# Two-part f32r queries and keys in row pairs, P @ V in halves, and keys loaded one by one, in a kernel of two gated attentions

## The chip, the cores and the metric

The kernel runs on one core of a Trainium2 chip. The metric is the time of one execution on the device, in microseconds (us). The profile is one execution taken by the hardware profiler. Its engines are PE (TensorE: matrix products, with weight loads shown apart as PEld), DVE (VectorE), ACT (ScalarE), POOL (GpSimd) and SP (SyncE, which here issues nearly all DMAs). A name such as L560 is line 560 of the kernel before.

## The reference

A sequence of 2048 tokens of width 512 passes through two attentions of 32 heads with 16 columns each, and the two results are mixed by a gate that belongs to the token.

```python
g = sigmoid((x * gate_w).sum(-1))                 # gate of a token
# A: full attention, no mask
q, k, v = heads(x @ wqkv)                         # 32 heads of 16
a = softmax(q @ k^T * 0.25) @ v @ wo_a            # 2048 x 2048 scores a head
# B: four segments of 512 tokens, each causal, with a running memory
for s in range(4):
    p = softmax(qs @ ks^T * 0.25 + causal_mask)   # 512 x 512
    a_mem = (phi(qs) @ M) / (phi(qs) @ z + 1e-6)
    o_s = sigmoid(beta) * a_mem + (1 - sigmoid(beta)) * (p @ vs)
    M, z = M + phi(ks)^T @ vs, z + sum(phi(ks))
b = concat(o_s) @ wo_b
out = g * a + (1 - g) * b
```

All tensors are float32, and the result has to be of float32 quality.

## The kernel before

**Parts of a number.** PE takes float32 slowly, so a float32 factor is split into parts of fewer bits, and a product is a sum over pairs of parts. In the projections both factors are two f32r parts (`h` and `l`), and three products (l·h, h·l, h·h) make one. In the scores q and k are each three bf16 parts, and the pairs of parts are laid out along the rows of one product: 16 rows for each of six pairs, 96 in all, and three more rows in which q carries the negative row maximum in three parts and k carries ones. A score product thus has 99 rows and gives the score less its row's maximum.

**Projections.** They run in slots (`slot`, L247). A slot is the twelve products (L250) of one tile, and it has four places at which posted functions run. For A there are four chunks of 512 tokens with twelve slots each: four tiles of q, four of k, four of v. B follows with the same slots. A tile of q or k (`qk_tile`, L283) is an octet of heads by 512 tokens. ACT writes its first part as `q1` (L294), DVE forms the rest (L301), ACT writes the second part `q2` (L307), DVE or POOL the third, `q3` (L315), and each part is stored to scratch in DRAM (`qd`, `kd`) by a DMA of its own (L295, L308, L316). The buffers of the parts are two deep. For B, phi of the tile is formed too and goes into the memory's products (`mem_q`, `mem_den`, `mem_k`). `load_gate` loads x by rows, and DVE forms the gate's logits beside A's slots; the gate's sigmoid (L401) and the DMAs that spread it (L404 to L407) come between A's and B's projections.

**Units and steps of the attention.** A unit is a group of four heads and a chunk of 512 queries. A has 8 groups by 4 chunks with 16 steps each (a step is a block of 128 keys), 512 steps. B has 32 units with 4 steps each, whose products are 512, 384, 256 and 128 columns wide because of the causal mask. The loop over steps is written out in order. A step runs four scores (`score_parts`, L560), each followed by an exponential on ACT (L563) into the tile `p`; one step of row maxima (`max_parts`) that runs ahead, by 22 steps in A and by 12 in B (`lead`); and P @ V (`values`, L579) of a step two (A) or three (B) steps back. The products of the maxima (L174 in A, L185 in B) have queries on the partitions, and DVE reduces each along its keys (L176, L190). When a unit's maxima are complete, `finish_max` splits them in parts on POOL, and `transpose_max` brings them into rows by a product (L154), an ACT copy (L156) and a DMA into the unit's q tile (L157). Scores have three PSUM banks, maxima three, P @ V one. P @ V has four heads in four column strips of the array; each product is in float32 and shows as two records in the profile. A score and a product of a maximum alternate on PE: score, maximum, score, maximum, and at the end of the step P @ V. At the end of a unit ACT copies the P @ V bank (L583) and SP stores it (L586).

**Loads.** All of the following go through SP's queue, in the order of the program. A unit's q tile takes three loads (`load_q`, L116 to L118), a key tile three (`load_k`, L125 to L127), of 48, 32 and 19 rows for k and 48, 32 and 16 for q. The row copies that the pairs need are made by these loads, for k with a repeated source. `loads` issues what a step of the maxima needs five steps (`PRE`) ahead. In A the four key tiles of a group are issued together with the first q tile of the group, ahead of it; in B a unit has one key tile and one q tile. There are buffers for six q tiles and eight key tiles. After each octet of A, its 2 MB of sums and inverse row sums are loaded (`a_load`) and stored again, scaled.

**Beside the steps.** Lists by step (`at`, `filler`) hold the scaling of A's and B's results and the output projection (L721), whose products run between the scores of B's steps. The first 22 steps of maxima run beside B's projections: `some_max` runs one product in places 1 and 3 of each slot from B's fourth slot (n = 3) on, and `loads(0)` ahead of B's first slot issues the first four key tiles and the first q tile.

Of the kernel before, what the change touches and what calls it, by code (L numbers as in the profile page):

```python
# [10 lines left out]
F32 = mybir.dt.float32  # L11
F32R = mybir.dt.float32r
BF16 = mybir.dt.bfloat16
# [27 lines left out]
def gated_mix(ctx, tc, x, xT, wqkv, a_wo, b_wq, b_wk, b_wv, b_wo, beta, gate_w, out):  # L41
# [3 lines left out]
    # ---------------------------------------------------------------- scratch in DRAM  # L45
    dr = ctx.enter_context(tc.tile_pool(name="dr", bufs=1, space=DRAM))
    # rows (split, d), heads of an octet, tokens of a chunk; three rows of ones below those of k
    qd = {}
    kd = {}
    for side in "AB":  # L50
        for o in range(NO):
            for c in range(NCH):
                qd[side, o, c] = dr.tile([48, 8, CH], BF16, name=f"qd{side}{o}{c}")
                kd[side, o, c] = dr.tile([51, 8, CH], BF16, name=f"kd{side}{o}{c}")
# [7 lines left out]
    # 32 rows a head: 16 of P @ V, then the sum of P  # L62
# [6 lines left out]
    # ---------------------------------------------------------------- constants  # L69
# [3 lines left out]
    identb = const.tile([128, 128], BF16, name="identb")  # L73
    nc.vector.tensor_copy(identb, identf)
# [15 lines left out]
    ones = const.tile([24, CH], BF16, name="ones")  # L90
# [4 lines left out]
    # ---------------------------------------------------------------- pools of the attention  # L95
# [7 lines left out]
    steps = []          # of the scores  # L103
# [6 lines left out]

    def load_q(u):
# [4 lines left out]
        nc.sync.dma_start(t[0:48], src[:, hs])  # L116
        nc.sync.dma_start(t[48:80], src[0:32, hs])
        nc.sync.dma_start(t[80:96], src[0:16, hs])  # L118
        qt[u] = t

    def load_k(side, g, c):
        t = kp.tile([128, 4, CH], BF16, tag="k", name=f"k{side}{g}{c}")
        src = kd[side, g // 2, c]
        hs = slice(4 * (g % 2), 4 * (g % 2) + 4)
        nc.sync.dma_start(t[0:48], src[0:16, hs].unsqueeze(0).broadcast_to([3, DH, 4, CH]))  # L125
        nc.sync.dma_start(t[48:80], src[16:32, hs].unsqueeze(0).broadcast_to([2, DH, 4, CH]))  # L126
        nc.sync.dma_start(t[80:99], src[32:51, hs])  # L127
        kt_[side, g, c] = t

    # ------------------------------------------------ row maxima, queries on partitions  # L130
    pmt = {}
    late = []           # (step of the maxima at which to run, function)

    def finish_max(u):
# [6 lines left out]
        ms = mp.tile([128, 3, 4, 4], BF16, tag="ms", name="ms")  # L141
        r1 = mp.tile([128, 4, 4], F32, tag="r1", name="r1")
        r2 = mp.tile([128, 4, 4], F32, tag="r2", name="r2")
        nc.gpsimd.tensor_copy(ms[:, 0], nm)  # L144
        nc.gpsimd.tensor_sub(r1, nm, ms[:, 0])
        nc.gpsimd.tensor_copy(ms[:, 1], r1)
        nc.gpsimd.tensor_sub(r2, r1, ms[:, 1])
        nc.gpsimd.tensor_copy(ms[:, 2], r2)
# [75 lines left out]
    with ExitStack() as p0:  # L224
# [270 lines left out]
        while posted:  # L495
            slot()
# [374 lines left out]
```

## Time and profile before

| what | us |
|---|---|
| three runs: lowest, median, highest | 2488.54, 2488.62, 2495.42 |
| the profiled execution, first to last instruction | 2486.5 |
| PE busy in it | 2180.2 |
| DVE busy | 1745.8 |
| ACT busy | 1470.8 |
| POOL busy | 294.5 |

The profiled execution has no other time than its span, which is 2.1 us below the median of the runs. A group of instructions in the profile is given by its line, engine and operation, by what it writes and reads, by its count, and by its busy time and the mean duration of one. A matmul's duration includes its way through the array, so that neighbours overlap: what a product costs PE is read from the distance between two starts. The granted clock is a share of PE's full clock.

### The profile page before, as it was taken

The page shows a single profiled execution, that of the slowest core. Times are in us where ns is not written, and L with a number is a line of the kernel's source. Part 1 is how long each engine was busy: PE and PEld are TensorE (multiplying, and loading weights), DVE is VectorE, ACT ScalarE, POOL GpSimd, SP SyncE. Part 2 cuts the span into 40 slices and gives each one's busy share as a digit, 9 for nine tenths or more (in the row PEclk, how much of TensorE's full clock was granted, in tenths as well). Part 3 has the DMA queues.
Part 4 walks back from the last instruction along what each step waited for, and adds up shares of the span by engine and source line. Part 5 has one row for each costly group of instructions (what it writes and reads, how often), then busy time and mean ns, then how long its engine had stood idle before and what let it go on. Part 6 is the DMA issues. An engine that isn't in the chain of part 4 may idle for free.

```text
span 2486.5 us, 33483 instructions
## 1 busy us (share of the span) xinstructions
PE 2180.2 (88%) x12033; PEld 840.2 (34%) x12033; DVE 1745.8 (70%) x3506; ACT 1470.8 (59%) x2853; POOL 294.5 (12%) x613
## 2 busy tenths in 40 slices
PE   8958999979979879989897997988999967687878
PEld 6745672222222222222222222222222222233335
DVE  5436668868868768877786886877788556565641
ACT  4433437657757657766675775766677844454543
POOL 3011120112000000000000000000000033232331
PEclk9988999989989989999998998999999988897999
DMA  6554431122110210010111001121001234344442
GB/s 204 191 170 129 147 114 44 68 95 69 56 42 13 63 37 23 20 36 22 47 43 43 12 12 37 32 63 36 22 21 31 74 102 116 121 114 131 116 134 91
DMA packets 98887, 182.96 MB, mean 74 GB/s; under 512 B 13392, under 2 KB 50032, under 8 KB 95904
## 3 DMA queue, kind: packets, MB, share of 16 engines
q1 hardware_dynamic: 97216, 179.41, 23.5%
q0 software_dynamic: 1504, 1.40, 0.3%
q8 instruction: 95, 1.56, 0.3%
q14 instruction: 72, 0.59, 0.1%
HBM read 112.72 MB, written 67.26 MB: 72 GB/s over the span
## 4 chain that ended last, share of the span: by engine, by line
PE 70%; DMA 22%; SPq 4%; DVE 1%; issue 1%; ACT 1%; POOL 1%; DVEq 0%; ACTq 0%; POOLq 0%
PE st L560 20%; PE ops L579 20%; PE sm L174 17%; PE pr L250 7%; DMA qB<-qdB 5%; DMA qA<-qdA 4%; DMA kB<-kdB 3%; PE fin L721 2%; DMA qA<-mt 2%; DMA qdA<-q 2%; PE sm L185 1%; SPq L126 1%; DMA vB<-vdB 1%; SPq L116 1%; SPq L127 1%
## 5 line engine op out<-in xcount | busy, mean ns | idle before, releaser
L563 ACT ACTIVATE p<-st 128x512 f32<-128x512 f32 (+1 forms) x2400 | 1247.8, 597 | 716.2 <-PE st L560 686.0
L176 DVE TENSOR_REDUCE pm<-sm 128x1 f32<-128x512 f32 x2048 | 1279.2, 683 | 383.7 <-PE sm L174 381.6
L174 PE MATMUL sm<-kA,qA 96*128 96x512 bf16 x2048 | 789.9, 386 | 148.7 <-DMA qA<-qdA 148.7
L560 PE MATMUL st<-qA,kA 99*128 99x512 bf16 x2048 | 787.5, 386 | 25.6 <-DMA qA<-mt 22.2
L579 PE MATMUL ops<-p,vA 128*17 128x512 f32 x4096 | 545.6, 605 | 0.0
L560 PEld LDWEIGHTS <-kA 99*128 99x128 bf16 x2048 | 200.5, 98 | 622.9 <-issue 417.4
L190 DVE CUSTOM_DVE_ANT_0 sm<-sm,cmask 128x256 f32<-128x256 f32 (+3 forms) x512 | 248.4, 507 | 183.7 <-PE sm L185 175.1
L174 PEld LDWEIGHTS <-qA 96*128 96x128 bf16 x2048 | 202.3, 99 | 358.6 <-DMA qA<-qdA 151.0
L185 PE MATMUL sm<-kB,qB 96*128 96x256 bf16 (+3 forms) x512 | 162.9, 332 | 100.4 <-DMA qB<-qdB 56.7
L144 POOL CAST ms<-nm 128x16 bf16<-128x16 f32 x64 | 14.1, 221 | 1425.0 <-DVE nm L138 1312.5
L560 PE MATMUL st<-qB,kB 99*128 99x256 bf16 (+3 forms) x512 | 164.1, 334 | 2.0 <-DMA qB<-mt 1.6
L579 PEld LDWEIGHTS ops<-p,vA 128*17 128x17 f32 x4096 | 68.1, 95 | 225.0 <-issue 224.4
L565 POOL TENSOR_SCALAR_AFFINE_SELECT p<-p 128x512 f32<-128x512 f32 x128 | 81.5, 637 | 277.4 <-ACT p L563 277.3
L579 PE MATMUL ops<-p,vB 128*17 128x512 f32 (+3 forms) x1024 | 101.6, 473 | 1.6 <-ACT oraw L583 0.8
L560 PEld LDWEIGHTS <-kB 99*128 99x128 bf16 x512 | 51.9, 102 | 131.0 <-issue 104.4
L185 PEld LDWEIGHTS <-qB 96*128 96x128 bf16 x512 | 53.4, 104 | 122.9 <-DMA qB<-qdB 103.1
L294 ACT CAST q<-pr 128x512 bf16<-128x512 f32 x64 | 37.4, 584 | 84.3 <-DMA qdB<-q 38.6
L190 DVE DVE_READ_ACCUMULATOR2_ANT pm<- 128x1 f32 x512 | 72.1, 141 | 0.0
L250 PE MATMUL pr<-xh,wql 128*128 128x512 f32 x128 | 58.2, 455 | 11.4 <-DVE wql L351 9.1
L301 DVE TENSOR_TENSOR r<-pr,q 128x512 f32<-128x512 f32 x64 | 43.8, 685 | 34.0 <-ACT q L294 32.0
L307 ACT CAST q<-r 128x512 bf16<-128x512 f32 x64 | 39.4, 616 | 35.5 <-DVE r L301 34.3
L315 POOL TENSOR_TENSOR q<-r,q 128x512 bf16<-128x512 f32 x32 | 37.3, 1168 | 168.0 <-ACT q L307 168.0
(140 smaller groups left out, 1497.6 us busy)
## 6 DMA issues: line engine op xcount, KB each, us to landing
odA<-oraw SPq DMA_DIRECT2D x32, 256.0 KB
odB<-oraw SPq DMA_DIRECT2D x32, 256.0 KB
raw<-xT SPq DMA_DIRECT2D x7, 1024.0 KB
qdA<-q SPq DMA_DIRECT2D x48, 128.0 KB
kdA<-q SPq DMA_DIRECT2D x48, 128.0 KB
kA<-kdA SPq DMA_DIRECT2D x32, 192.0 KB
qA<-qdA SPq DMA_DIRECT2D x32, 192.0 KB
qdB<-q SPq DMA_DIRECT2D x48, 128.0 KB
```

The source lines that it names most:

```text
L174: nc.tensor.matmul(ps, q[0:96, h, s * 128:(s + 1) * 128], kt_[side, g, j][0:96, h, :], start=True, stop=True)
L176: nc.vector.tensor_reduce(pm[:, h, s, j:j + 1], ps, axis=AX.X, op=ALU.max)
L185: nc.tensor.matmul(ps[:, n0:n0 + n], q[0:96, j, s * 128:(s + 1) * 128], kt_[side, g, c][0:96, j, :n], start=True, stop=True)
L190: nc.vector.tensor_tensor_reduce(r, r, cmask[:, CH - n:], 1.0, -3.0e38, ALU.add, ALU.max, pm[:, j - per + 1 + e, s, 0:1])
L250: nc.tensor.matmul(ps, l(a, k), r(b, k), start=(n == 0), stop=(n == 11))
L301: nc.vector.tensor_sub(r, ps, q1)
L307: nc.scalar.copy(q2, r)
L560: nc.tensor.matmul(ps[:, h % per, :n], k[0:99, h, b * 128:(b + 1) * 128], q[0:99, h, q0:], start=True, stop=True)
L563: nc.scalar.activation(p[:, h - per + 1:h + 1, :n], ps[:, :, :n], AF.Exp, scale=SCALE)
L565: nc.gpsimd.affine_select(out=p[:, :, 0:128], in_=p[:, :, 0:128], pattern=[[0, 4], [1, 128]], base=0, channel_multiplier=-1, compare_op=AL ...
L579: nc.tensor.matmul(ops[32 * h:32 * h + 17, q0:], v[h], p[:, h, :n], start=(i == 0), stop=(i == last), tile_position=(0, 32 * h))
L721: nc.tensor.matmul(ps, l[:, o], r[:, o], start=(n == 0), stop=(n == 23))
```

## The change

- **q and k in two f32r parts.** `qk_tile` writes `q1` on ACT and `q2` on DVE, and stores two f32 parts where it stored three of bf16. The third part and its store are gone. A score's or a maximum's product has three pairs of 16 rows, 48 rows, and two more for the maximum (`finish_max` makes two parts of it).
- **Row pairs.** Heads 0 and 1 of a group lie at partitions 0 to 49 of the tile, heads 2 and 3 at partitions 64 to 113 (`rows`). In a step of A the scores go through heads 0 to 3 and the maxima between them through heads 2, 3 and then 0, 1, so that a score and its neighbouring maximum use different halves. Of the keys, a step of the maxima takes two chunks for one head of each pair.
- **Loads.** A q tile takes four loads (32 and 16 rows for each half), a key tile four (32 and 18), the rows of the maxima two.
- **P @ V in two halves.** In A, half of the columns run ahead of the third score and half at the end of the step. In B, P @ V runs ahead of the fourth score. The products of the output projection run behind the step and not between its scores.
- **Keys one by one.** The four key tiles of the next group are issued at steps 30, 36, 42 and 52 of a group's 64.
- **First maxima late, in pairs.** `some_max` starts with slot 22 of B and runs two products at a place, of different row halves.
- **The gate.** `load_gate` and the logits move beside B's slots, and the gate's sigmoid and its DMAs behind the last of them.
- **Small ones.** For products of 256 columns or fewer, a bank now holds two heads; before, it held four of 128 columns.

```diff
-LATE_T = 3          # steps from the last maximum of a unit to its transposition
-PRE = 5             # steps by which loads run ahead of the maxima
+LATE_T = 3
+PRE = 5
+K_AHEAD = (30, 36, 42, 52)
...
     def load_q(u):
         side, g, c = u
-        t = qp.tile([128, 4, CH], BF16, tag="q", name=f"q{side}{g}{c}")
+        t = qp.tile([128, 2, CH], F32R, tag="q", name=f"q{side}{g}{c}")
         src = qd[side, g // 2, c]
-        hs = slice(4 * (g % 2), 4 * (g % 2) + 4)
-        nc.sync.dma_start(t[0:48], src[:, hs])
-        nc.sync.dma_start(t[48:80], src[0:32, hs])
-        nc.sync.dma_start(t[80:96], src[0:16, hs])
+        for r in range(2):
+            hs = slice(4 * (g % 2) + 2 * r, 4 * (g % 2) + 2 * r + 2)
+            nc.sync.dma_start(raw(t)[64 * r:64 * r + 32], src[0:32, hs])
+            nc.sync.dma_start(raw(t)[64 * r + 32:64 * r + 48], src[0:16, hs])
         qt[u] = t
 
     def load_k(side, g, c):
...
-        nc.sync.dma_start(t[0:48], src[0:16, hs].unsqueeze(0).broadcast_to([3, DH, 4, CH]))
-        nc.sync.dma_start(t[48:80], src[16:32, hs].unsqueeze(0).broadcast_to([2, DH, 4, CH]))
-        nc.sync.dma_start(t[80:99], src[32:51, hs])
+        for r in range(2):
+            hs = slice(4 * (g % 2) + 2 * r, 4 * (g % 2) + 2 * r + 2)
+            nc.sync.dma_start(raw(t)[64 * r:64 * r + 32], src[0:16, hs].unsqueeze(0).broadcast_to([2, DH, 2, CH]))
+            nc.sync.dma_start(raw(t)[64 * r + 32:64 * r + 50], src[16:34, hs])
         kt_[side, g, c] = t
 
+    def rows(t, h, n):
+
+        return t[64 * (h // 2):64 * (h // 2) + n, h % 2]
...
         def part(j):
             if side == "A":
                 ps = sm_ps.tile([128, CH], F32, tag="sm", name="sm")
-                h, s = i // 4, i % 4
-                nc.tensor.matmul(ps, q[0:96, h, s * 128:(s + 1) * 128], kt_[side, g, j][0:96, h, :],
+                h, s, kc = (2 if j < 2 else 0) + i // 8, i // 2 % 4, 2 * (i % 2) + j % 2
+                nc.tensor.matmul(ps, rows(q[:, :, s * 128:(s + 1) * 128], h, 48), rows(kt_[side, g, kc], h, 48),
                                  start=True, stop=True)
...
             if i == 0:
-                if side == "A" and c == 0:
+                if u == ("A", 0, 0):
                     for k in range(NCH):
                         load_k("A", g, k)
...
+            if side == "A" and g + 1 < NG and c * 16 + i in K_AHEAD:
+                load_k("A", g + 1, K_AHEAD.index(c * 16 + i))
...
             def e1():
-                nc.vector.tensor_sub(r, ps, q1)
+                nc.vector.tensor_sub(q2, ps, q1.bitcast(F32))
+                nc.sync.dma_start(dst[16:32].rearrange("d h t -> h d t"), raw(q2))
...
             def e2():
-                nc.scalar.copy(q2, r)
-                nc.sync.dma_start(dst[16:32].rearrange("d h t -> h d t"), q2)
...
-            def e3():
-                (nc.gpsimd if side == "B" else nc.vector).tensor_sub(q3, r, q2)
-                nc.sync.dma_start(dst[32:48].rearrange("d h t -> h d t"), q3)
...
-            parts.pop(0)()
+            parts.pop(0)()
+            parts.pop(len(parts) // 2)()
...
-        for n in range(3, 64):
+        for n in range(22, 64):
             for place in (1, 3):
                 posted.setdefault((s0 + n, place), []).append(lambda: some_max(0))
...
+            nc.tensor.matmul(ps[:, h % per, :n], rows(k[:, :, b * 128:(b + 1) * 128], h, 50),
+                             rows(q[:, :, q0:], h, 50), start=True, stop=True)
...
+        a, b = (0, n) if half is None else (half * n // 2, (half + 1) * n // 2)
         for h in range(4):
-            nc.tensor.matmul(ops[32 * h:32 * h + 17, q0:], v[h], p[:, h, :n], start=(i == 0), stop=(i == last),
-                             tile_position=(0, 32 * h))
+            nc.tensor.matmul(ops[32 * h:32 * h + 17, q0 + a:q0 + b], v[h], p[:, h, a:b], start=(i == 0 and a == 0),
+                             stop=(i == last and b == n), tile_position=(0, 32 * h))
...
         for h in range(4):
+            for w in done if side == "A" and h == 2 else []:
+                values(w, 0)
+            for w in done if side == "B" and h == 3 else []:
+                values(w)
             ss[h]()
-            for f in mm[h * per:(h + 1) * per] + ff[h * pf:(h + 1) * pf]:
+            for f in mm[h * per:(h + 1) * per]:
                 f()
+        for w in done if side == "A" else []:
+            values(w, 1)
...
+        for f in fill.get(t, []):
+            f()
```

More of the change, by code (lines that the diff above doesn't have):

```diff
@@ L12 @@
 F32R = mybir.dt.float32r
-BF16 = mybir.dt.bfloat16
 AF = mybir.ActivationFunctionType
@@ L153, in transpose_max @@
         pt = pool.tile([128, CH], F32, tag=tag, name="mt_ps")
[L154 to L157 removed]
+        nc.tensor.matmul(pt[:32, :128], ms.rearrange("p r a h s -> p (r a h s)"), identr, start=True, stop=True)
+        mt = mp.tile([32, 128], F32R, tag="mt", name="mt")
+        nc.scalar.copy(mt, pt[:32, :128])
+        for r in range(2):
+            nc.sync.dma_start(raw(qt[u])[64 * r + 48:64 * r + 50], raw(mt)[16 * r:16 * r + 16])
     def max_parts(m):
@@ L566, in part, with values @@
                                         base=0, channel_multiplier=-1, compare_op=ALU.is_ge, fill=0.0)
-        return [lambda h=h: part(h) for h in range(4)]
-    def values(t):
+        order = range(4)
+        return [lambda h=h: part(h) for h in order]
+    def values(t, half=None):
         (side, g, c), i = steps[t]
-        p = pt_.pop(t)
+        p = pt_[t]
         if side == "A":
```

101 lines of the change are left out of this document (46 added, 55 removed).

## The prediction

> **What bounds the kernel now.** I read the table of stretches first, cut where the work changes, then the waits of the longest stretch, then one step of it in the timeline, then the chain of waits where a stretch stalls.
>
> ```profile
> 0.00:152.70 152.70, 139.30 (x577) 110.97 (x577) 74.79 (x132) 65.25 (x113) 23.47 (x53) 1.00 0.65 205
> 152.70:203.40 50.70, 16.36 (x64) 11.94 (x65) 9.25 (x16) 10.97 (x22) 6.59 (x11) 0.66 0.34 114
> 203.40:373.40 170.00, 169.72 (x795) 119.77 (x794) 122.79 (x214) 75.68 (x139) 34.65 (x38) 1.00 0.41 131
> 373.40:1984.10 1610.70, 1470.62 (x8171) 430.51 (x8170) 1262.75 (x2133) 1084.53 (x2114) 81.40 (x212) 0.95 0.14 41
> 1984.10:2440.50 456.40, 350.20 (x2273) 141.32 (x2276) 263.85 (x987) 224.24 (x447) 145.22 (x298) 0.87 0.40 118
> 2440.50:2486.50 46.00, 33.98 (x161) 25.67 (x154) 12.39 (x26) 10.14 (x21) 3.16 (x3) 0.93 0.26 94
> ```
>
> The columns are stretch, length, then busy time and count of PE, PEld, DVE, ACT and POOL, granted clock, DMA share, GB/s. The stretches are: first projections; a stall at the start of the second projections; the rest of them; the attention of A (two thirds of the time); the attention of B; the tail. In A, PE is busy for 1470.62 of 1610.70 us. One step of A in the timeline shows why:
>
> ```profile
> 1202.11 0.39 PE L560 MATMUL st<-qA,kA 99*128 99x512 bf16 x1
> 1202.33 0.38 PE L174 MATMUL sm<-kA,qA 96*128 96x512 bf16 x1
> 1202.53 2.06 ACT L563 ACTIVATE p<-st 128x512 f32<-128x512 f32 x4 [0.77 <-PE st L560]
> 1202.75 2.48 DVE L176 TENSOR_REDUCE pm<-sm 128x1 f32<-128x512 f32 x4 [0.35 <-PE sm L174]
> ...
> 1203.64 0.38 PE L174 MATMUL sm<-kA,qA 96*128 96x512 bf16 x1
> 1203.95 0.13 PEld L579 LDWEIGHTS ops<-p,vA 128*17 128x17 f32 x8 [0.43 <-issue]
> 1203.95 1.05 PE L579 MATMUL ops<-p,vA 128*17 128x512 f32 x8
> 1204.94 0.39 PE L560 MATMUL st<-qA,kA 99*128 99x512 bf16 x1
> ```
>
> A step lasts from 1202.11 to 1204.94, 2.83 us. PE issues eight products 0.22 us apart (1202.11, 1202.33), 1.74 us, and P @ V takes the other 1.08: 0.99 from its first product to the next score (1203.95 to 1204.94), and 0.09 because it starts 0.31 and not 0.22 after the last product. ACT needs 2.06, and sits idle 0.77 on scores. DVE needs 2.48 and sits idle 0.35 on products: in A, PE bounds, and DVE is next, 0.35 behind.
>
> ```profile
> L560 PE MATMUL st<-qA,kA x2048: 376/379/634, 373.4 to 1983.7; 99*128 99x512 bf16 x187
> ```
> ```profile
> PE sm L174 <- DMA qA<-qdA: 114.4, 7, 17.0
> ...
> PEld L560 <- DMA qA<-mt: 25.0, 3, 8.8
> ```
>
> 2048 scores are 512 steps; 512 x 2.83 is 1449 us, so 162 of A's 1610.7 are stalls. Seven are at the group changes (114.4 us of waiting on the first q of a group, some 130 with the slow-clock products behind each), three wait for the maxima rows on their way into the q tile (some 32).
>
> **The change, part by part.** *Row pairs.* Each product now has 48 or 50 rows of f32r, at partition 0 or 64, and neighbours in the order (score, maximum) lie in different row halves. Their writes go to different banks. What the trace has of f32r products and of products that share the array:
>
> ```profile
> 242.99 1.39 PE pr L250 x6
> ```
> ```profile
> L250 PEld LDWEIGHTS pr<-xh,wqh x128: 187/188/338, 6.0 to 344.0; 128*128 128x128 f32 x128
> ```
> ```profile
> L579 PE MATMUL ops<-p,vA 128*17 128x512 f32 x4096 | 545.6, 605 | 0.0
> L176 DVE TENSOR_REDUCE pm<-sm 128x1 f32<-128x512 f32 x2048 | 1279.2, 683 | 383.7 <-PE sm L174 381.6
> ```
>
> An f32r product costs 0.232 us (1.39 / 6); its weight load lasts 0.188 and is hidden under the product before. Four products of P @ V, in four column strips, overlap: 4096 of 0.605 would be 2478 us and took 545.6. No row shows two row halves at work together. So the eight products of a step cost between 4 x 0.232 = 0.93 (full overlap) and 8 x 0.232 = 1.86 (none). I take 0.93, since the nearest row of a divided array, that of the column strips, shows full overlap. [...]
>
> *P @ V in halves.* Its price for 256 columns stands in B:
>
> ```profile
> 2108.92 0.63 PE L579 MATMUL ops<-p,vB 128*17 128x256 f32 x8
> 2109.48 0.28 PE L560 MATMUL st<-qB,kB 99*128 99x256 bf16 x1
> ```
>
> 0.56 to the next score, with the 0.09 of entry 0.65 a half, 1.30 a step where it was 1.08: 0.22 us a step more for PE, the price of leaving and entering the divided array twice as often.
>
> *A step.* PE: 0.93 + 1.30 = 2.23, and at each of the two returns to row pairs a weight load of 0.188 instead of 0.10 that nothing covers, 0.18: 2.41. DVE: four reductions at (2.48 - 0.683) / 3 = 0.60 each, 2.40. ACT: 2.06. Two engines within 0.01 of each other, coupled by three banks each way, will not both be full; I take 2.50, so 512 x 2.50 = 1280. Bounds: 2.40 (DVE alone) to 1.86 + 1.30 + 0.18 = 3.34.
>
> *Keys one by one.* Before a group's first maximum SP issues twelve key loads, then three of q:
>
> ```profile
> 471.54 0.75 SPq L125
> ...
> 491.73 2.31 SPq L116
> 494.08 16.03 DMA qA<-qdA
> ```
>
> 38.6 us from 471.54 to landing at 510.1, against a lead of five steps (14 us). Now a key tile is issued every 6 to 10 steps, 15 us or more apart, for its part of that work (99 of 492 rows of 4 KB, 8 us), into buffers that the group before last has left long ago; q comes alone, in four loads instead of three. The seven stalls go: -130. Cover: the lead of at least 12 steps behind the last key tile. The maxima rows go in two transfers of half the rows instead of one:
>
> ```profile
> 812.85 15.54 DMA qA<-mt
> ```
>
> That landed late because the loads of an octet (2 MB) stood before it; these stay where they are. Three such stalls stay, 32 us and some 4 more, since three steps of lead are now shorter by 1 us. The new P @ V half in the middle of a step meets the copy of the last unit's sums 0.5 us earlier than now; some 0.25 us a unit (half of that, an estimate), 32 units, 8 us. A: 1280 + 36 + 8 = 1324 instead of 1610.7.
>
> *Projections.* Each tile of q or k loses an ACT cast and a subtraction and stores two f32 parts for three bf16 ones. In the first projections PE already runs without gaps (139.30 busy of 152.70, the rest at the start): nothing, both ways. At the start of the second:
>
> ```profile
> 155.58 0.79 SPq L125
> ...
> 167.32 20.66 DMA kA<-kdA
> 188.03 12.85 DMA qdB<-q
> ```
>
> The sixteen key loads and four of q stay in this place, of the same bytes, so B's first q tiles still leave only when they are through, at about 201, and the PSUM tiles behind them hold PE: -2. That the first maxima (88 products) wait until the 23rd slot and run four a slot costs PE 22 x 2 pairs of 0.53 (0.232, two changes of division of 0.1, a bare load of 0.1) = 23, where they cost 44 slots x 2 x 0.22 = 19: +4. The gate's tail (a transposition, a sigmoid, small DMAs) now comes after the last slot:
>
> ```profile
> 156.46 0.51 POOL L404 DMA_DIRECT2D gd<-gt  x1 [32.57 <-ACT gt L401]
> ...
> 163.07 0.63 POOL L405 DMA_DIRECT2D gA<-gd  x1 [5.26 <-DMA gd<-gt]
> ```
>
> Only a buffer of the attention that takes the place of gt could wait for it, 0 to 7 (156.46 to 163.07); I take 0, since four tiles of P stand to take turns and the gates themselves are read tens of steps later. The four loads of x move to a stretch with DMA share 0.41. Sum 375 for 373.4.
>
> *B.* PE idles 106 of 456.4 us, on loads:
>
> ```profile
> PE sm L185 <- DMA qB<-qdB: 56.7, 14, 9.1
> ```
> ```profile
> 2106.26 0.71 SPq L125 DMA_DIRECT2D kB<-kdB  x1
> ...
> 2116.33 0.80 SPq L157 DMA_DIRECT2D qB<-mt  x1
> ```
>
> SP issues one more load of k, of q (0.7 each) and of the maxima rows (0.8) for each of 32 units, 2.2 x 32 = 70 if all of it delays the loads. Against that PE's products of a unit (eight each of 0.22, 0.17, 0.11, 0.06: 4.5 us) halve, 2.2 x 32 = 70 if all of it lies on the path. Bounds -106 (no idle time left) to +70; between them I take a third of the gain, -22, and none of the loss, since PE is busy for 77% of B, some of it behind late loads, and SP has pauses of microseconds between the rows shown: 434. The smaller edits (fillers behind the step, two exponentials where one did four 128-column heads, three fewer POOL steps per maximum) meet engines busy less than 60% of B: 0. The tail keeps 46.
>
> Sum of the profiled execution: 375 + 1324 + 434 + 46 = 2179 for 2486.5. The median of the runs is 2488.62, 2.1 above the span; with it 2181.
>
> **The rivals.** (1) *Weight loads take turns.* Two halves want two loads per 0.232 us; if each holds the one way in for its 0.188, eight cost 1.50, the step is 1.50 + 1.30 = 2.80, A is 512 x 2.80 + 44 = 1478, total 2335. For it: 0.188 is near 0.232 already. Against: eight small loads of P @ V stand within 0.13 us in the timeline.
>
> (2) *A load waits for the product in its own rows.* Then a half repeats 0.188 + 0.232 = 0.42, four times 1.68, the step is 2.98, A 1570, total 2427. Against: in the full array a load does run under a product in the same rows, since six products take 1.39 us and not 6 x 0.42. [...]
>
> (3) *The halves do not overlap (slower).* Eight products in turn, 1.86 + 1.30 = 3.16 and 3.34 with the bare loads: A 1662 to 1754, total 2519 to 2611. It decides from a step of 3.10 us on: (2488.6 - 2.1 - 375 - 434 - 46 - 44) / 512 = 3.10. For it: no row shows row halves together. Against: the column strips do.
>
> (4) *The keys' early loads do not help*, because q or the maxima rows queue behind a key tile instead: the seven stalls stay, 2181 + 130 = 2311. Against: 8 us of transfer in 15 us of time.
>
> (5) *The new key loads land sooner.* The fifteen loads of a group are 492 rows of 4 KB, 2.0 MB in 38.6 us, 52 GB/s, where the first projections moved 205: something in how these loads are cut holds them back, and they are cut anew (48, 32 and 19 rows become 32, 18, 32 and 18). [...] Against: bytes and rows are the same. [...]
>
> **How the numbers follow.** My forecast (pairs overlap, a step of 2.40 to 2.65, loads as fast as now) 0.40; (1) 0.13; (2) 0.06; (3) 0.15; (4) 0.06; (5), with the forecast's step, 0.20. The time is the forecast's, 2181; its own range, from 2.40 to 2.65 a step, is 2130 to 2258. The range for all leaves out (3), 0.15, and 0.05 below, where (5) meets a step of 2.40: 2080 to 2430. A measurement tells 0.3% from no change here. Faster 0.83 (all but (3), less 0.02 for a (2) that comes out dearer); the same 0.02; slower 0.15.
>
> **What would show it.** In A's timeline: pairs of products starting together, a step of 2.40 to 2.65 us, DVE's waits on products near zero and its busy share near 95%; the group-change wait gone from the list of waits; three waits on the maxima rows left. PE's step of 3.1 or more, with starts 0.23 apart, would be rival (3). [...]

## The result, and the profile after

The changed kernel takes 2172.84 us (median; 2172.06 to 2183.93) where the kernel before, on the same chip, takes 2490.32: a ratio of 0.873 (95% interval 0.871 to 0.876). The forecast was 2181. The profiled execution has a span of 2170.4 us. In the lines of after, L182 and L184 are the product and the reduction of A's maxima, L195 and L200 those of B's, L566 and L569 a score and its exponential, L588 P @ V, L262 the projections' products, and L304 and L311 the two parts of q and k.

The table of stretches of after, cut where the work changes as it was for before (stretch, length, busy time and count of PE, PEld, DVE, ACT, POOL, granted clock, DMA share, GB/s):

```profile
0.00:164.70 164.70, 139.32 (x577) 110.52 (x577) 43.45 (x68) 45.93 (x81) 22.94 (x54) 0.97 0.63 191
164.70:204.30 39.60, 14.30 (x60) 10.98 (x60) 7.35 (x13) 9.11 (x18) 0.33 (x1) 0.71 0.43 144
204.30:385.20 180.90, 179.88 (x799) 124.50 (x799) 130.61 (x248) 62.63 (x111) 1.44 (x5) 0.99 0.53 168
385.20:1704.20 1319.00, 1285.81 (x12255) 468.56 (x12258) 1239.60 (x2136) 1131.91 (x2116) 62.95 (x115) 0.98 0.17 51
1704.20:2122.30 418.10, 384.45 (x2273) 184.94 (x2273) 256.69 (x985) 222.40 (x480) 128.01 (x211) 0.74 0.43 130
2122.30:2170.40 48.10, 34.78 (x158) 26.42 (x158) 12.39 (x26) 9.90 (x21) 3.17 (x3) 0.93 0.23 85
```

| stage | before | forecast | after |
|---|---|---|---|
| projections | 373.4 | 375 | 385.2 |
| attention of A | 1610.7 | 1324 | 1319.0 |
| attention of B | 456.4 | 434 | 418.1 |
| tail | 46.0 | 46 | 48.1 |

A carries the gain, and its time came as forecast, to 5 us. The projections got longer instead of staying, and B got shorter by more than was forecast, at a granted clock of 0.74 instead of 0.87. One step of A in the timeline of after:

```profile
1301.71 4.94 DVE L184 TENSOR_REDUCE pm<-sm 128x1 f32<-128x512 f32 x8 [0.19 <-PE sm L182]
...
1302.37 0.49 PE L566 MATMUL st<-qA,kA 50*128 50x512 f32 x1
...
1302.37 0.49 PE L182 MATMUL sm<-kA,qA 48*128 48x512 f32 x1
1302.47 0.19 PEld L566 LDWEIGHTS st<-qA,kA 50*128 50x128 f32 x1
1302.48 0.19 PEld L182 LDWEIGHTS sm<-kA,qA 48*128 48x128 f32 x1
1302.70 0.39 PE L566 MATMUL st<-qA,kA 50*128 50x512 f32 x1
1302.70 0.39 PE L182 MATMUL sm<-kA,qA 48*128 48x512 f32 x1
...
1303.03 0.63 PE L588 MATMUL ops<-p,vA 128*17 128x256 f32 x8
...
1303.58 0.49 PE L566 MATMUL st<-qA,kA 50*128 50x512 f32 x1
```

A score and its maximum start at the same 1302.37: row halves work at once. The weight loads for the next pair (PEld, 1302.47 and 1302.48) run side by side, under the products of this one. From pair to pair it is 0.33, to P @ V 0.33, and from there to the next pair 0.55, in sum 1.21 for half a step; the median distance between steps is 2.44. DVE does eight reductions without a pause in 4.94 us, (4.94 - 0.685) / 7 = 0.61 each with 0.685 the mean duration of one, so four of them fill 2.43: the two engines tie, as forecast, and DVE is busy for 1239.60 of 1319.00 us, 94%. The waits of after:

```profile
DVE pm L184 <- PE sm L182: 53.5, 55, 8.8
...
DVE q L311 <- DMA qdA<-q: 44.7, 16, 5.6
...
ACT q L304 <- DMA qdA<-q: 34.8, 11, 4.9
...
PE st L566 <- DMA qA<-mt: 24.9, 3, 8.5
PE sm L195 <- DMA qB<-qdB: 24.4, 11, 7.8
```

DVE's wait on products is 53.5 where it was 381.6, the group-change wait is gone, and the three waits on the maxima rows are there. The waits of DVE and ACT on the stores of q's parts in the first projections have grown to more than double.

### The profile page after: what moved, and what is told of

The parts are those of the page before. It is cut to its first block, busy times and chain, and to the rows that moved or that the text cites. A ratio compares the mean times of both kernels' runs of the same rounds, so it can differ in the third digit from the quotient of the medians.

```text
span 2170.4 us, 41503 instructions
## 1 busy us (share of the span) xinstructions
PE 2038.5 (94%) x16113; PEld 925.9 (43%) x16113; DVE 1690.1 (78%) x3474; ACT 1481.9 (68%) x2823; POOL 218.8 (10%) x389
## 4 chain that ended last, share of the span: by engine, by line
PE 71%; DMA 18%; DVE 5%; ACT 3%; SPq 1%; issue 1%; DVEq 0%; ACTq 0%
PE st L566 31%; PE ops L588 27%; PE pr L262 6%; DMA qB<-qdB 3%; DVE pm L184 3%; PE fin L733 3%; DMA kB<-kdB 3%; DMA qdA<-q 2%; DMA qA<-mt 2%; DMA odB<-oraw 2%; PE sm L182 2%; ACT p L569 2%; DMA kdA<-q 1%; DMA inv<-rdB 1%; DMA kA<-kdA 1%
## 5 line engine op out<-in xcount | busy, mean ns | idle before, releaser
L569 ACT ACTIVATE p<-st 128x512 f32<-128x512 f32 (+2 forms) x2432 | 1301.5, 585 | 371.2 <-PE sm L195 123.4
L184 DVE TENSOR_REDUCE pm<-sm 128x1 f32<-128x512 f32 x2048 | 1255.3, 685 | 63.0 <-PE sm L182 53.5
L566 PE MATMUL st<-qA,kA 50*128 50x512 f32 x2048 | 758.3, 450 | 27.8 <-DMA qA<-mt 24.9
L182 PE MATMUL sm<-kA,qA 48*128 48x512 f32 x2048 | 758.6, 455 | 0.7 <-DVE pm L184 0.5
L588 PE MATMUL ops<-p,vA 128*17 128x256 f32 x8176 | 651.7, 391 | 5.2 <-ACT oraw L595 5.2
L566 PEld LDWEIGHTS st<-qA,kA 50*128 50x128 f32 x2048 | 306.7, 187 | 458.3 <-ACT p L569 413.7
L200 DVE CUSTOM_DVE_ANT_0 sm<-sm,cmask 128x256 f32<-128x256 f32 (+3 forms) x512 | 244.3, 513 | 146.4 <-PE sm L195 88.2
L182 PEld LDWEIGHTS sm<-kA,qA 48*128 48x128 f32 x2048 | 314.0, 187 | 25.1 <-DVE pm L184 12.2
L588 PEld LDWEIGHTS ops<-p,vA 128*17 128x17 f32 x8176 | 135.9, 95 | 370.6 <-issue 350.8
L195 PE MATMUL sm<-kB,qB 48*128 48x256 f32 (+3 forms) x512 | 181.3, 452 | 32.9 <-DMA qB<-qdB 24.4
L566 PE MATMUL st<-qB,kB 50*128 50x256 f32 (+3 forms) x512 | 185.2, 453 | 0.8 <-ACT p L569 0.2
L566 PEld LDWEIGHTS st<-qB,kB 50*128 50x128 f32 x512 | 104.1, 239 | 135.1 <-issue 66.0
L311 DVE TENSOR_TENSOR q<-pr,q 128x512 fp32r<-128x512 f32 x64 | 44.0, 688 | 135.2 <-DMA qdA<-q 44.7
L304 ACT CAST q<-pr 128x512 fp32r<-128x512 f32 x64 | 37.5, 585 | 131.0 <-PE pr L262 36.9
L588 PE MATMUL ops<-p,vB 128*17 128x512 f32 (+3 forms) x1024 | 123.5, 564 | 0.0
L195 PEld LDWEIGHTS sm<-kB,qB 48*128 48x128 f32 x512 | 102.0, 237 | 45.6 <-issue 28.3
L200 DVE DVE_READ_ACCUMULATOR2_ANT pm<- 128x1 f32 x512 | 72.4, 141 | 0.0
L262 PE MATMUL pr<-xh,wql 128*128 128x512 f32 x128 | 56.0, 438 | 13.5 <-DVE wql L356 6.5
L262 PE MATMUL pr<-wkh,xl 128*128 128x512 f32 x64 | 29.8, 465 | 25.3 <-DVE q L311 25.3
L262 PE MATMUL pr<-xl,wqh 128*128 128x512 f32 x128 | 51.4, 402 | 0.0
```

The lines of the kernel that those rows point to most:

```text
L182: nc.tensor.matmul(ps, rows(q[:, :, s * 128:(s + 1) * 128], h, 48), rows(kt_[side, g, kc], h, 48), start=True, stop=True)
L184: nc.vector.tensor_reduce(pm[:, h, s, kc:kc + 1], ps, axis=AX.X, op=ALU.max)
L195: nc.tensor.matmul(ps[:, n0:n0 + n], rows(q[:, :, s * 128:(s + 1) * 128], h, 48), rows(kt_[side, g, c][:, :, :n], h, 48), start=True, stop ...
L200: nc.vector.tensor_tensor_reduce(r, r, cmask[:, CH - n:], 1.0, -3.0e38, ALU.add, ALU.max, pm[:, h - per + 1 + e, s, 0:1])
L262: nc.tensor.matmul(ps, l(a, k), r(b, k), start=(n == 0), stop=(n == 11))
L304: nc.scalar.copy(q1, ps)
```

## The experiments

Ratios are to the kernel before, measured beside it on the same chip. Differences to the changed kernel are differences of the two ratios, times 2490 us.

### What makes a step of A: halves at once, and P @ V in two

**Both products of a pair in one half** (`same_half`, in the changed kernel):

```diff
-                h, s, kc = (2 if j < 2 else 0) + i // 8, i // 2 % 4, 2 * (i % 2) + j % 2
+                h, s, kc = (0 if j < 2 else 2) + i // 8, i // 2 % 4, 2 * (i % 2) + j % 2
```

> The changed kernel with the maxima of A taken in the other order of heads, so that a score and the maximum beside it lie in the same row half. If the gain of A comes from row halves working together, each half step loses two overlaps of 0.232 us: 1.22 becomes 1.68 us, a step 3.37 instead of 2.44, some 460 to 480 us more, about 2640 us. If the gain has another source (48 rows instead of 96, the order of the steps, the loads), the step stays near 2.44 and the time near 2173 us.

It took 3878.61 us, ratio 1.558 (1.551 to 1.565), far beyond every expectation. The stretch of A, and a part of its timeline:

```profile
386.60:3410.90 3024.30, 3022.10 (x12261) 1310.29 (x12260) 1401.87 (x2139) 1247.53 (x2117) 62.60 (x115) 0.50 0.08 22
```
```profile
1502.01 0.62 PE L182 MATMUL sm<-kA,qA 48*128 48x512 f32 x1
1502.01 0.33 PEld L566 LDWEIGHTS st<-qA,kA 50*128 50x128 f32 x1
...
1502.43 0.62 PE L566 MATMUL st<-qA,kA 50*128 50x512 f32 x1
...
1502.86 0.62 PE L182 MATMUL sm<-kA,qA 48*128 48x512 f32 x1
```

Products in the same rows now run one after another, so the overlap of the changed kernel is real and comes from the row halves. But they stand 0.43 apart and not 0.23: PE is busy for 3022.10 of 3024.30 us, and the granted clock is 0.50 throughout. The clock, not the lost overlap alone, makes the 3879. Behind the first product of a half step the loads of the next weights are hidden even here, in the same rows: the load for the product at 1502.43 begins at 1502.01, with the product ahead, and since twice the 0.23 of an f32r product is 0.46, products 0.43 apart leave no room for it. So this load did not wait for the product in its own rows, and rival 2 falls.

**Is it the rows that set the clock?** (`one_part`) The kernel before, with each score and maximum cut to rows of the upper half:

```diff
-                nc.tensor.matmul(ps, q[0:96, h, s * 128:(s + 1) * 128], kt_[side, g, j][0:96, h, :],
+                nc.tensor.matmul(ps, q[64:96, h, s * 128:(s + 1) * 128], kt_[side, g, j][64:96, h, :],
...
-            nc.tensor.matmul(ps[:, h % per, :n], k[0:99, h, b * 128:(b + 1) * 128], q[0:99, h, q0:],
+            nc.tensor.matmul(ps[:, h % per, :n], k[64:99, h, b * 128:(b + 1) * 128], q[64:99, h, q0:],
```

> The kernel before, but each score and each maximum uses rows 64 to 98 or 64 to 95 of its tiles alone instead of 0 to 98 or 0 to 95, so two thirds of the terms of q.k are left out and the output is another; number, columns and type of the products and all loads stay. Theory A (the granted clock follows the rows at work, as in the run with both products of a pair in one half): the clock in A falls from 0.95 to about 0.5, a step from 2.83 to 5 or 6 us, 3700 to 4000. Theory B (that run's slow clock comes from f32r products in turn, not from rows): 2480 to 2500.

4243.46 us, 1.706 (1.703 to 1.710):

```profile
393.50:3507.80 3114.30, 3113.60 (x8180) 489.39 (x8180) 1403.03 (x2138) 1245.24 (x2115) 81.05 (x212) 0.50 0.07 21
```
```profile
1500.73 0.10 PEld L174 LDWEIGHTS <-qA 32*128 32x128 bf16 x1 [0.44 <-issue]
1500.73 0.60 PE L174 MATMUL sm<-kA,qA 32*128 32x512 bf16 x1
...
1501.27 0.60 PE L560 MATMUL st<-qA,kA 35*128 35x512 bf16 x1
```

The same number of bf16 products with the same columns, fewer rows: PE never idles, and the clock falls from 0.95 to 0.50. So neither f32r nor idle time sets it here: from the kernel before to this one, only the rows at work differ, and the values with them. The expectation's upper end, 4000, was passed because the products stand 0.54 apart, 0.10 more than twice the 0.22 of before. The tenth is the weight load: here 4069 of the 4096 loads of scores and maxima in A begin with their own product, as at 1500.73, and not with the product ahead, as all but 597 do in the kernel before. Why loads in the same rows are bare here and hidden in `same_half` (35 and 32 rows in turn perhaps) was not tried. They do not explain the clock, which is 0.50 in `same_half` too, where 1112 of 4096 are bare.

**P @ V whole again** (`v_whole`, in the changed kernel):

```diff
-            for w in done if side == "A" and h == 2 else []:
-                values(w, 0)
...
-            values(w, 1)
+            values(w)
```

> The changed kernel with P @ V of a step of A whole at the end of the step. PE saves one round trip between the divisions of the array, 0.22 us a step. If PE alone sets the step of 2.44 us, it falls to DVE's 2.40 and the time to about 2153 us. If the three banks of the maxima couple PE and DVE, so that the fourth product waits for the first reduction and P @ V runs behind it, the step is about 2.5 us and the time about 2200 us.

2288.50 us, 0.920 (0.917 to 0.923): 116 us slower than the changed kernel. A step in its timeline:

```profile
1302.99 0.39 PE L566 MATMUL st<-qA,kA 50*128 50x512 f32 x1
...
1303.19 2.07 ACT L569 ACTIVATE p<-st 128x512 f32<-128x512 f32 x4 [0.65 <-PE sm L182]
1303.22 2.48 DVE L184 TENSOR_REDUCE pm<-sm 128x1 f32<-128x512 f32 x4 [0.24 <-PE sm L182]
...
1303.84 0.49 PE L566 MATMUL st<-qA,kA 50*128 50x512 f32 x1 [0.21 <-ACT p L569]
...
1304.40 1.05 PE L588 MATMUL ops<-p,vA 128*17 128x512 f32 x8
```

PE runs through three pairs faster than ACT and DVE can use them, then has no bank: the fourth score (1303.84) waits until the first exponential has left its bank. P @ V comes behind it as one block of 1.0 us, and in that block both other engines run dry (idle 0.65 and 0.24 at the start of the step shown, behind the block of the step before). The step is 2.72, A 1431 us. The two halves spread the pairs over the step.

**The halves in the kernel before** (`before_halves`):

```diff
+            for w in done if side == "A" and h == 2 else []:
+                values(w, 0)
             ss[h]()
...
+        for w in done if side == "A" else []:
+            values(w, 1)
```

> The kernel before, with P @ V of A in two halves of 256 columns, the first before the third score, the second at the end of the step; nothing else of the change. Theory A (the prediction's term, 1.30 us a step instead of 1.08, on the engine that bounds): 0.22 x 512 = 113 slower, 2600. Theory B (the halves save as such, as taking them out of the changed kernel cost 115 us): 2380 to 2490.

2587.92 us, 1.040 (1.038 to 1.043), 101 us slower; the median step goes from 2.833 to 3.067. That is 0.23 a step, the prediction's term (0.22) to a hundredth. So the same edit costs 101 where PE alone bounds, and saves 116 where the pairs are there.

### The keys

**All four keys of a group together again** (`keys_together`, in the changed kernel), **and the keys one by one in the kernel before** (`before_keys`):

```diff
-                if u == ("A", 0, 0):
+                if side == "A" and c == 0:
...
-            if side == "A" and g + 1 < NG and c * 16 + i in K_AHEAD:
-                load_k("A", g + 1, K_AHEAD.index(c * 16 + i))
```

(The second is the reverse of it in the other kernel.)

> The changed kernel with the four key tiles of a group issued together ahead of the group's first q, as before. If these loads take what they took before (38.6 us a group against a lead of now 12.2 us), seven stalls of some 25 us return: about 2350 us. If the new key loads are faster by three tenths (27 us a group), the stalls are some 15 us each: about 2280 us. If loading keys one by one brought nothing, 2173 us.

> The kernel before with nothing but the keys of the next group loaded one by one. By the sum of the prediction the seven group stalls go, 130 us: about 2360 us. If the transfers only move their wait to the q or the maxima rows behind them, 2400 to 2490 us.

`keys_together`: 2292.33, 0.920 (0.916 to 0.925), 117 slower than the changed kernel. `before_keys`: 2353.73, 0.946 (0.943 to 0.948), 136 faster than before. In the list of waits of the first the group changes are back:

```profile
PE sm L182 <- DMA qA<-qdA: 69.5, 7, 10.9
```

69.5 us in seven waits where the kernel before had 114.4 in seven: the new loads land sooner, but together they still come too late. The prediction's 130 is borne out by the second; rival 4 falls.

Taken together: keys alone take the kernel to 2354, the pairs and all the rest without halves to 2289, the halves to 2173. The 65 us of the middle step are not the pairs' alone, since the projections and B change with them. In A, where the pairs and halves work, the stretch is 1477.8 us in `before_keys`, 1431.2 in `v_whole` and 1319.0 in after: pairs without halves are worth 47 us there, pairs with halves 159.

### The projections and B's loads

**A key's repeated rows by two loads** (`key16`, in the changed kernel):

```diff
-            nc.sync.dma_start(raw(t)[64 * r:64 * r + 32], src[0:16, hs].unsqueeze(0).broadcast_to([2, DH, 2, CH]))
+            for e in range(2):
+                nc.sync.dma_start(raw(t)[64 * r + 16 * e:64 * r + 16 * e + 16], src[0:16, hs])
```

> The changed kernel, but the two copies of a key's first sixteen rows in the tile come by two loads of 16 rows instead of one load with a repeated outermost count of 2; bytes the same, one issue of SP (0.7 us) more for each half of a key tile. [...] Theory B (SP's issues or the memory set the pace): 32 more issues of 0.7 before the second projections' stores get their turn, and 2 x 0.7 a unit in B: 2173 to 2220.

2138.37, 0.859 (0.856 to 0.863), 35 faster than the changed kernel. SP's queue at the start of the second projections, first key load and first store of q, in after:

```profile
167.53 0.68 SPq L131 DMA_DIRECT2D kA<-kdA  x1
...
194.22 0.63 SPq L305 DMA_DIRECT2D qdB<-q  x1
```

and in this kernel, with its stretch of B:

```profile
170.32 0.96 SPq L132 DMA_DIRECT2D kA<-kdA  x2
...
187.66 0.59 SPq L306 DMA_DIRECT2D qdB<-q  x1
```
```profile
1700.90:2093.70 392.80, 373.28 (x2268) 179.85 (x2264) 255.09 (x984) 220.26 (x478) 127.48 (x211) 0.75 0.46 137
```

17.3 us instead of 26.7, with half as many issues again and the same bytes (17.0 and 26.8 in `combo` and `three_bufs`, below), so SP's issues did not set the pace; B goes from 418 to 393. The load with an outermost count of 2 was the slow one. A key tile that is loaded alone in A says the same: from its first issue to its last packet in the trace it takes 10.9 us in `before_keys` (issued at 410.93), 7.9 in after (425.75) and 4.4 here (419.96). What makes a load with that count slow was not shown.

**Three buffers for the parts of q and k** (`three_bufs`, in the changed kernel):

```diff
-            q1 = wk.tile([128, CH], F32R, tag="q1", name="q1")
-            q2 = wk.tile([128, CH], F32R, tag="q2", name="q2")
+            q1 = wk.tile([128, CH], F32R, tag="q1", name="q1", bufs=3)
+            q2 = wk.tile([128, CH], F32R, tag="q2", name="q2", bufs=3)
...
```

To make room, two tiles of the memory's products (`am` and `pt`) have one buffer instead of two in this run.

> The changed kernel with three buffers instead of two for each of the two f32 parts of q and k in the projections (one instead of two for two small tiles, to make room). Theory A (in the first projections ACT and DVE wait for a store to leave its buffer, 44.7 + 34.8 + 23.0 + 21.4 us, and PE behind them): the first projections fall from 164.7 to 153 or 156: 2160 to 2165. Theory B (the stores themselves are what cannot keep up, so a third buffer only fills later): within 4 us of 2173.

2162.02, 0.870 (0.867 to 0.872), whose interval touches the changed kernel's 0.871 to 0.876, so that the gain of some 10 us is not clear by the times alone. Its first projections and the rest of its second ones:

```profile
0.00:157.60 157.60, 138.38 (x576) 111.18 (x577) 43.71 (x68) 46.01 (x81) 22.92 (x54) 0.97 0.63 200
...
171.70:379.10 207.40, 180.69 (x799) 124.18 (x798) 129.11 (x246) 62.19 (x110) 1.76 (x6) 0.94 0.51 163
```

The first projections lose 7 us. In the profiles of all eight kernels here with two f32 buffers they take 164.7 to 173.2, in the two with three (this one and `combo`, below) 157.6 and 152.6. That the stores hold the buffers is so; but most of the stall of the second projections only moves to a later slot: A starts at 379.1 instead of 385.2.

**The first maxima early and singly** (`early_single`, in the changed kernel):

```diff
             parts.pop(0)()
-            parts.pop(len(parts) // 2)()
...
-        for n in range(22, 64):
+        for n in range(3, 64):
```

> The changed kernel, but with the first maxima singly, two a slot from the fourth slot of the second projections on, as the kernel before has them. Theory A (each change between full and half array costs, so a pair is the cheaper): 88 products of 0.45 to 0.53 (40 to 47 us) for 44 pairs of 0.65 (29): 11 to 18 slower, 2184 to 2191. Theory B (a pair in a late slot costs more than it saves, by banks and DVE at that place): 5 to 10 faster, 2163 to 2168.

2207.15, 0.886 (0.883 to 0.890), 32 slower. In its timeline one maximum alone, and in that of after a pair, between products of the projections:

```profile
300.71 0.39 PE L262 MATMUL pr<-xh,wvh 128*128 128x512 f32 x1
301.03 0.50 PE L182 MATMUL sm<-kA,qA 48*128 48x512 f32 x1
301.46 0.66 PE L435 MATMUL tps<-identf,ph 128*128 128x128 f32 x4
```
```profile
300.19 0.40 PE L262 MATMUL pr<-wkh,xh 128*128 128x512 f32 x1
300.52 0.50 PE L182 MATMUL sm<-kA,qA 48*128 48x512 f32 x2
300.95 0.50 PE L262 MATMUL pr<-wkh,xl 128*128 128x512 f32 x1
```

From the last full product to the next thing on PE it is 0.75 for one and 0.76 for two, of which 0.23 is the full product itself: 0.52 for one half-array product and 0.53 for a pair. The full product that follows has a bare load too and keeps PE for 0.33 instead of 0.23 (300.95 to the next at 301.28). With that a single costs 0.63 and a pair 0.64 (medians of the 48 and 17 that stand between two products of the projections): the second one is free. 88 x 0.63 is 55 and 44 x 0.64 is 28, so some 27 of the 40 us by which the two profiled spans differ. 5 lie in a longer stall of the second projections (44.9 for 39.6), 4 in the first projections and 2 in B (420.2 for 418.1).

### The maxima rows, and the clock of B

**An octet's sums in four pieces** (`aload`, in the changed kernel):

```diff
-        nc.sync.dma_start(big(("Ar", o), "raw"), odA[o][:, 0:16])
-        nc.sync.dma_start(big(("Ai", o), "inv"), heads(rdA[o], S))
+        cs = slice(c * CH, (c + 1) * CH)
+        nc.sync.dma_start(held["Ar", o][:, c], odA[o][:, 0:16, cs])
+        nc.sync.dma_start(held["Ai", o][:, c], heads(rdA[o][:, cs], CH))
...
-        at(t0 + 8, lambda o=o: a_load(o))
-            at(t0 + 13 + 2 * c, lambda o=o, c=c: a_mul(o, c))
-        at(t0 + 21, lambda o=o: a_store(o))
+            at(t0 + 9 + 3 * c, lambda o=o, c=c: a_load(o, c))
+            at(t0 + 14 + 3 * c, lambda o=o, c=c: a_mul(o, c))
+        at(t0 + 25, lambda o=o: a_store(o))
```

> The changed kernel, but the 2 MB of an octet's sums are loaded in four pieces, three steps apart, and each is used five steps later, instead of at once. Theory A (the three waits on the maxima rows in A come from these loads standing ahead of them in the queue): the three stalls of 10.5 to 11 us and the slow-clock products behind each, 44 us in all, go: 2128 to 2140. Theory B (the maxima rows are late by another cause): three stalls stay, 2173.

2132.11, 0.857 (0.855 to 0.859), 41 faster than the changed kernel. The wait on the maxima rows is gone, and A's stretch is

```profile
394.80:1672.60 1277.80, 1268.93 (x12259) 464.20 (x12258) 1238.51 (x2138) 1131.81 (x2117) 63.29 (x115) 1.00 0.18 52
```

at the full clock, 41 us shorter: three stalls of 8 us had cost 41 with the slow-clock steps behind them.

**Work added to hold B's clock** (`warm`, in the changed kernel). B of after, cut at its slow part; the output's products begin in the third row:

```profile
1704.00:1788.00 84.00, 73.66 (x435) 33.09 (x434) 53.01 (x214) 44.47 (x96) 23.86 (x42) 0.65 0.36 104
1788.00:1874.00 86.00, 79.87 (x408) 36.15 (x409) 53.80 (x217) 41.72 (x90) 22.12 (x41) 0.50 0.47 143
1874.00:1960.00 86.00, 81.94 (x538) 41.69 (x536) 59.64 (x223) 49.34 (x107) 27.91 (x47) 0.90 0.46 142
```

```diff
+    def warm():
+        ps = ms_ps.tile([128, D], F32, tag="ms", name="warm")
+        w = wos["B"][0][:, 0]
+        for n in range(2):
+            nc.tensor.matmul(ps, w[:, 0:128], w, start=(n == 0), stop=(n == 1))
+    for t in range(nA + 2, nA + 49):
+        filler(t, warm)
```

> The changed kernel, with two products more of the full array (128 rows, 512 columns, f32r, of weights that are there already, into a bank that nobody reads) at the end of each of 47 steps of B's attention before the output's products begin: work added, none taken away. Theory A (B's first 170 us run at a granted clock of 0.5 to 0.65 since only half-array products come there): the clock there rises to 0.85 or more, and this stretch gets 15 to 40 us shorter: 2130 to 2158. Theory B (the stretch goes by its loads, or the clock by something else): 47 x (0.46 + 0.2) = 31 slower, up to 2204.

2185.46, 0.878 (0.876 to 0.881): no gain, 12 slower.

```profile
1704.00:1880.00 176.00, 163.56 (x979) 72.62 (x975) 113.00 (x440) 89.67 (x193) 45.98 (x84) 0.76 0.39 121
```

Full-array products do raise the clock, to 0.76 where the two rows of after average 0.57 (B starts at 1709.1 in this run, so that the row's first 5 us are still A's). But the added products use up what the clock gives: B takes 429.2 us for 418.1. Neither theory had both.

### The three gains together

`combo` is the changed kernel with the edits of `key16`, `three_bufs` and `aload`.

> The three edits that each made the changed kernel faster, together: the keys' rows by two loads of 16, three buffers for the projections' parts, the octets' sums in four pieces. If the three gains (34, 11 and 41 us) lie in different places of the program, they add: 2087. If the third buffer only moves the wait to the start of the second projections, or key loads and octet pieces now collide: 2100 to 2130.

2075.06 us, 0.836 (0.833 to 0.839): 93 us below the changed kernel, where the three gains sum to 85, which is the same within the runs' intervals, and faster than both kernels. Its stretches up to the end of B:

```profile
0.00:152.60 152.60, 137.16 (x576) 111.34 (x577) 43.71 (x68) 46.14 (x81) 22.90 (x54) 0.98 0.65 206
152.60:166.80 14.20, 14.20 (x61) 11.22 (x62) 8.36 (x14) 9.10 (x18) 0.00 (x0) 1.00 0.61 174
166.80:361.70 194.90, 180.36 (x801) 124.31 (x799) 129.22 (x246) 62.44 (x111) 1.76 (x6) 0.96 0.54 173
361.70:1642.40 1280.70, 1271.77 (x12260) 464.21 (x12259) 1239.03 (x2138) 1131.71 (x2117) 63.04 (x115) 0.99 0.19 52
1642.40:2021.90 379.50, 364.25 (x2268) 177.40 (x2264) 254.03 (x983) 219.11 (x478) 128.24 (x211) 0.79 0.47 142
```

The first projections are back at the 152.7 of before, and A starts 23.5 us sooner than in after. Here the faster key loads keep short the stall that `three_bufs` only moved: the second projections take 209.1 us in all, where they take 221.5 there. B is 39 us shorter, 13 more than by the key loads alone; what the other two edits do for B was not taken apart.

## Why the prediction was right

2181 was forecast, 2173 came, and the mechanism of A is right: pairs overlap, and keys loaded one by one end the group stalls. That the number is as near as 8 us is in part luck. The errors of the four stages (+10, -5, -16, +2) nearly cancel, those inside A and inside B partly cancel too, and the forecast's own condition "loads as fast as now" did not hold.

- **Row pairs**: right. Pairs start together; `same_half` shows that without the halves the products run in turn. Rivals 1 and 2 fall: the two loads of a pair run side by side (1302.47 and 1302.48) and under products in the same rows, and a pair follows a pair after 0.33, less than the 0.376 of two loads in turn. Rival 3's price was worked out at the full clock; the run that has its condition costs 3879, not 2519 to 2611, because the clock falls as well (0.50 in A). So the risk on the slow side was larger than the prediction had it.
- **P @ V in halves, 0.22 a step for PE**: right as a price (0.23 in `before_halves`), incomplete as an account. The prediction treated the halves as a cost only. That they keep three banks from running full and empty (`v_whole`, 116 us) was not in the sum; it only shows in that the step came at 2.44, near its lower bound of 2.40, and not at 2.72.
- **A step of 2.50**: the median is 2.44, so 512 of them are 31 us less than the sum had: the two tied engines fill nearly all of it. Against that, some 28 us lie in longer steps. The step in which a unit's sums are copied takes 2.70, which is the 8 us of the sum; but the step with the transposition of the maxima and one more of each unit take 2.61, and the first steps of A up to 4.7, 20 us that were not in the sum. The three stalls with the slow steps behind them cost 41 (`aload`) where 36 were forecast. -31, +20 and +5 make A's -5, and the mean step without stalls is 2.50 (1277.8 / 512 in `aload`), for another reason than the one given.
- **Keys one by one, -130**: right; -136 in the kernel before (`before_keys`).
- **First projections, "nothing, both ways"**: wrong, +12. The step said that PE runs without gaps and looked no further. The two f32 stores of a tile are 256 KB each where three of 128 KB went before, from buffers still two deep. In before the same wait stood, small and hidden:

```profile
DVE q L315 <- DMA qdA<-q: 19.2, 7, 4.9
ACT q L294 <- DMA qdA<-q: 15.9, 5, 4.5
```

  After has 44.7 and 34.8, and for k 23.0 and 21.4 more. The step that failed is "nothing": a wait that is hidden has slack, and the slack was not compared with a third more bytes and two instructions fewer a tile.
- **Start of the second projections, -2**: the stretch of the stall went from 50.7 to 39.6, -11. "Of the same bytes" was the wrong measure; the cut of the loads counted, as rival 5 had it: a key tile takes 7.9 us where it took 10.9, and `key16`, the same bytes cut again, takes another 10 off the stretch (29.6). The size at which rival 5 sets the range's lower end, 2080, is shown by no run; the runs show these 3.0 us a key tile and 11 us of the stretch. What moving the gate's work out of this place did was not tried alone.
- **Late maxima, +4**: the rest of the second projections took 10.9 more. Up to the next product a pair is 0.53, as forecast; the sum left out that the product behind it then has a bare load. With it a pair is 0.64, 28 in all, where a single product in the kernel before costs 0.24 between two of the projections' (88 of them 21): +7 of the 10.9. The rest was not traced to an end.
- **The gate's tail, 0**: the waits of after on it are POOL's own (44.3) and 0.6 of DVE's.
- **B, -22**: -38 came, by two errors in opposite directions. The loads landed sooner (PE's wait on q is 24.4 for 56.7, and its 17.5 on k are gone), which is rival 5; and the clock fell from 0.87 to 0.74, which no step had priced. In the trace of after the granted clock has two values, 1.00 (1882 to 1921, for one) and 0.50 (1791 to 1869), so that 0.74 is half the clock for about half of B ((1 - 0.74) / 0.5 x 418 = 217 us). What the clock cost and what the loads gave was not measured apart. So rival 5, given as another outcome than the forecast, came in part together with it.

## What to carry to other kernels

Products that use half the rows are worth trying in pairs of both halves: here the second was free (0.64 us for a pair, 0.63 for one), and in turn in one half they ran at a clock of 0.50 (`same_half`). What was gained on PE here was only kept because the long block between them, P @ V, was cut so that the banks of the other engines neither fill nor empty (116 us in `v_whole`); the same cut was a loss where PE alone bounds (101 us in `before_halves`). And an edit that changes bytes per store (+12 us in the first projections) or the outermost count of a load (35 us in `key16`) is priced at the buffer that waits for it, however well that wait is hidden now.

## What the runs showed of the hardware that was not expected

- The granted clock was 0.50 with PE busy all the time: 3022 of 3024 us with f32r products of 48 and 50 rows in turn (`same_half`), 3114 of 3114 with bf16 products of 32 and 35 rows (`one_part`). With 96 and 99 rows A ran at 0.95 (before) to 0.99 (`before_keys`), stalls included, with two halves at once at 0.97 (`three_bufs`) to 1.00 (`aload`), and at 0.93 in `keys_together`, whose group stalls are in the figure.
- B of after, with narrower pairs, ran at 0.65 and 0.50 (1704 to 1874) until full-array products of the output came in, then at 0.90 (1874 to 1960). What share of the array at what width holds the clock is open.
- Entering and leaving the divided array cost some 0.4 us here around a product, bare weight loads included, whether one or two products were inside (0.63 in `early_single` and 0.64 in after in all, of which 0.23 is a product).
- A weight load was hidden under a product in the same rows (six products of the full array in 1.39 us in before; half-array products 0.43 apart in `same_half`) or bare in the same rows (35 and 32 rows in `one_part`, products 0.54 apart); what decides is open.
